# State copies, score steps and the last stores of a fused retention and GELU kernel: a change of places

What was changed: the copies of the states of the later chunk pair were put in the second half of a block, some pairs of score products were issued one step later, and in the last tile the rows of batches 2 and 3 (its half u = 0, "even half") were stored whole instead of in two halves of columns.

## The chip, the cores and the metric

One core of one Trainium2 chip. The metric is the time of one execution in microseconds of device time; lower is better. A profile gives a span some 1.7 us shorter than the timed run it belongs to. Runs that took over 1.5% longer than the fastest of their kernel would count as slow; all runs told of here are in the fast state, except one single run of unknown state that is marked where it is told.

## The reference

Eight batches of eight-head attention with a causal decay in place of a softmax, then a two-layer MLP with the tanh form of GELU on all 4608 rows:

```python
def _attn_ref(q, k, v):                    # q, k, v: (8, 8, 576, 64)
    scores = scale * np.matmul(q, k.transpose(0, 1, 3, 2))
    gamma = 1.0 - 2.0 ** (-5.0 - np.arange(H))
    Dmat = np.where(rel >= 0, gamma[:, None, None] ** rel[None, :, :], 0.0)
    return np.matmul(scores * Dmat[None], v)

def _moe_ref(x, w_in, w_out):              # x: (4608, 512), w_in: (512, 2048)
    h = x @ w_in
    g = 0.5 * h * (1.0 + np.tanh(c * (h + 0.044715 * h * h * h)))
    return g @ w_out
```

## The kernel before

The retention is done in chunks of 128 rows with a running state. Each batch has four whole chunks and a tail of 64 rows. The MLP works through nine blocks `t` of 512 rows: eight of whole chunks, and a last one (t = 8) that gathers the tails. A block of t = 2 to 7 has 30 steps: 16 "up" steps (four 128x512 matmuls, then a GELU on ACT), then 14 "product" steps for the second layer, which is computed as seven half-size products of sums (a Strassen scheme), each for two halves `u`. Between steps, the attention of batch t + 1 is woven in, at step numbers that a table fixes:

```python
    def states(t, u, b, c, tag):                  # states of chunks c and c + 1
        def go():
            us = bank(tag, "us")
            for n in range(2):
                state(b, c + n, us, n)            # 8 matmuls
            for n in range(2):
                scan(b, c + n)                    # DVE: running state "ws"
        at(t, u, go)
        def sp(n, hl):                            # ACT: state into tbd / tbt, a copy of 0.40 us
            at(t, u + 2 + 2 * n + hl, lambda: spread(b, c + n, A.copy, (hl,)))
        ...
    def values(t, u, *xs):
        at(t, u, lambda: ([av(*x) for x in xs], [inter(*x[:2]) for x in xs]))
        for n, x in enumerate(xs):                # ACT: values into xT, which frees a PSUM bank
            at(t, u + 1 + n, lambda x=x: put(*x[:2]))
    ...
    for t in range(1, 7):
        b, e = t + 1, t - 3
        if t == 1:
            ...
            u0, u1, u2, u3 = 11, 17, 19, 25
            states(t, u0, b, 0, "B")
            scores(t, u0, (b, 0, ("t0", "t1")), (b, 1, ("t2", "A")))
        else:
            u0, u1, u2, u3 = (8, 14, 19, 25) if t == 2 else (7, 13, 19, 25) if t == 3 else (6, 12, 19, 25)
            ...
            scores(t, u0, (b, 0, ("t0", "t1")), (b, 1, ("t2", "A" if t > 2 else "C")), *tail)
        states(t, u1, b, 2, "t0")
        values(t, u1, (b, 0, "t1"), (b, 1, "t2"), ...)
        scores(t, u2, (b, 2, ("hp", "hp")), (b, 3, ("t1", "t2")))
        if t < 6:
            states(t, u3, b + 1, 0, "t0")
        values(t, u3, (b, 2, "t1"), (b, 3, "t2"))
```

The products of the second half need activation sums that DVE makes from the GELU outputs; product 6 is the first that needs the second sum:

```python
    nc.vector.tensor_tensor(out=s["1"], in0=a21, in1=a22, op=ALU.add)            # L488
    nc.vector.tensor_tensor(out=s["2"], in0=s["1"], in1=a11, op=ALU.subtract)    # L489
```

The stores of the last tile, one 64-row half per queue:

```python
        def end(o, i, v, d=slice(0, DM)):
            b = 4 * v + 2 * i
            for h, e in enumerate((nc.sync, nc.scalar)):
                r0 = S * (b + h) + M0
                e.dma_start(out=out[r0 : r0 + TL, d], in_=o[TL * h : TL * h + TL, d])
        ...
        elif m == 7:
            ...
            if last:
                add(keep["o1"][:, u, HD:DM], keep["u3"][:, u], keep["o1"][:, u, HD:DM])
                end(keep["o1"][:, u], 1, u, slice(HD, DM))
        ...
        elif m == 4:
            if last:
                add(keep["o1"][:, u, 0:HD], keep["s1"][:, u], pr("B")[:, u])
                end(keep["o1"][:, u], 1, u, slice(0, HD))
```

Lines that come up in the profile: L317 score matmuls, L338 states, L359 state copies, L367 and L388 values, L405 value copies, L415 up matmuls, L421 their GELU, L488 and L489 the activation sums, L508 products, L523 adds of products, L536 stores of the last tile.

Of the kernel before, what the change touches and what calls it, by code (L numbers as in the profile page):

```python
# [19 lines left out]
def kernel(  # L20
# [12 lines left out]
    NT, DM = out.shape  # L33
# [30 lines left out]
    def bank(tag, name, dt=F32):  # L64
        if tag == "att":
            tag = "t" + str(turns["n"] % 3)
            turns["n"] += 1
        return ps.tile([128, 512 if dt == F32 else 1024], dt, tag=tag, name=name, bufs=BUFS[tag])
# [130 lines left out]
    for h in range(H):  # L199
        u = 64 * (h % 2)  # L200
# [132 lines left out]
    def state(b, c, us=None, n=0):  # L333
        a = att[b]
        us = bank("att", "us") if us is None else us
        for p in range(HP):
            for hl in range(2):
                nc.tensor.matmul(  # L338
                    us[64 * hl : 64 * hl + 64, 256 * n + 64 * p : 256 * n + 64 * p + 64],
                    a["k"][:, col(c, p, hl)],  # L340
                    a["v"][:, col(c, p, hl)],
                    start=True, stop=True,
                )
        a["U", c] = us[:, 256 * n : 256 * n + 256]

    def scan(b, c):
        a = att[b]
        uc = a.pop(("U", c)).rearrange("p (q d) -> p q d", d=64)
        if c > 0:
            s = sb.tile([128, HP, 64], F32, tag="vs", name="vs", bufs=2)  # L350
            nc.vector.tensor_tensor(out=s, in0=uc, in1=a["w"], op=ALU.add)
            uc = s
        a["w"] = a["w", c] = w = sb.tile([128, HP, 64], F32, tag="ws", name="ws", bufs=2)
        nc.vector.tensor_tensor(out=w, in0=uc, in1=gt, op=ALU.mult)  # L354

    def spread(b, c, cp, hls=(0, 1)):
        for hl in hls:
            r = slice(64 * hl, 64 * hl + 64)
            cp(out=(tbd[b % 2][r, c, :, r] if c < NC - 1 else tbt[b % 4][r, :, r]), in_=att[b]["w", c][r])  # L359
# [85 lines left out]
    def ost():  # L445
        return sb.tile([128, 2, DM], F32, tag="ost", name="ost", bufs=2)
# [17 lines left out]
    HD = DM // 2  # L464
# [48 lines left out]
    keep = {}  # L513

    def after(t, m, u):
        last = t == NTB - 1
        if u == 0 and not (last and m in (6, 7, 4)):
            return
        us = slice(u, u + 1) if last and m in (6, 7, 4) else slice(0, 2)
        def pr(tag):  # L520
            return op[tag, u].rearrange("p (u d) -> p u d", u=2)
        def add(o, a, b):
            nc.vector.tensor_tensor(out=o, in0=a, in1=b, op=ALU.add)  # L523
        def send(o, i):
            if t < B:
                nc.sync.dma_start(
                    out=out[S * t : S * t + TB, :].rearrange("(u i p) d -> p u i d", u=2, i=2)[:, :, i, :], in_=o
                )
                return
            for v in range(2):  # L530
                end(o[:, v], i, v)
# [5 lines that stand above are left out]
        if m == 1:  # L537
            keep["s1"] = sb.tile([128, 2, HD], F32, tag="k1", name="k1", bufs=1)
            nc.scalar.copy(out=keep["s1"], in_=pr("A"))
        elif m == 6:  # L540
            if us.start == 0:
                keep["u2"] = sb.tile([128, 2, HD], F32, tag="k2", name="k2", bufs=1)
            add(keep["u2"][:, us], keep["s1"][:, us], pr("B")[:, us])
        elif m == 7:
            if us.start == 0:
                keep["u3"] = sb.tile([128, 2, HD], F32, tag="k3", name="k3", bufs=1)
            add(keep["u3"][:, us], keep["s1"][:, us], pr("B")[:, us])
            if last:
                add(keep["o1"][:, u, HD:DM], keep["u3"][:, u], keep["o1"][:, u, HD:DM])
                end(keep["o1"][:, u], 1, u, slice(HD, DM))  # L550
                return
            keep["o1"] = ost()
            add(keep["o1"][:, :, HD:DM], keep["u3"], pr("C"))
        elif m == 5 and last:
            keep["o1"] = ost()
            nc.scalar.copy(out=keep["o1"][:, :, HD:DM], in_=pr("C"))
        elif m == 2:
            keep["o0"] = ost()
            nc.scalar.copy(out=keep["o0"][:, :, 0:HD], in_=pr("A"))  # L559
        elif m == 3:  # L560
            add(keep["o0"][:, :, HD:DM], keep["u2"], pr("C"))
            send(keep["o0"], 0)
        elif m == 4:
            if last:
                add(keep["o1"][:, u, 0:HD], keep["s1"][:, u], pr("B")[:, u])
                end(keep["o1"][:, u], 1, u, slice(0, HD))
            else:
                add(keep["o1"][:, :, 0:HD], keep["s1"], pr("B"))
                send(keep["o1"], 1)
# [25 lines left out]
    V, P, A = nc.vector, nc.gpsimd, nc.scalar  # L595
# [48 lines left out]
    def at(t, u, f):  # L644
        if t > 0 and u > 29:
            t, u = t + 1, u - 30
        events.setdefault((t, u), []).append(f)
# [31 lines left out]
    def scores(t, u, *xs):  # L679
        at(t, u, lambda: [score(*x) for x in xs])  # L680

    def states(t, u, b, c, tag):
        def go():
            us = bank(tag, "us")
            for n in range(2):
                state(b, c + n, us, n)
            for n in range(2):
                scan(b, c + n)
        at(t, u, go)
        def sp(n, hl):  # L690
            at(t, u + 2 + 2 * n + hl, lambda: spread(b, c + n, A.copy, (hl,)))
        for n in range(2):
            for hl in range(2):
                sp(n, hl)

    def values(t, u, *xs):
        at(t, u, lambda: ([av(*x) for x in xs], [inter(*x[:2]) for x in xs]))
        for n, x in enumerate(xs):
            at(t, u + 1 + n, lambda x=x: put(*x[:2]))
# [7 lines left out]
    def turns_of(t, u, b, c, tag):  # L707
        at(t, u, lambda: turn(b, c, A.copy, tag))
# [9 lines left out]
    for t in range(1, 7):  # L718
        b, e = t + 1, t - 3
        if t == 1:  # L720
            for c, (u, tag) in enumerate(((7, "t2"), (9, "A"), (15, "C"), (17, "hp"))):
                turns_of(t, u, b, c, tag)
            u0, u1, u2, u3 = 11, 17, 19, 25
            states(t, u0, b, 0, "B")
            scores(t, u0, (b, 0, ("t0", "t1")), (b, 1, ("t2", "A")))
        else:
            u0, u1, u2, u3 = (8, 14, 19, 25) if t == 2 else (7, 13, 19, 25) if t == 3 else (6, 12, 19, 25)
            tail = [(e, NC, ("B", "C"))] if e >= 0 else []
            scores(t, u0, (b, 0, ("t0", "t1")), (b, 1, ("t2", "A" if t > 2 else "C")), *tail)
        states(t, u1, b, 2, "t0")  # L730
        values(t, u1, (b, 0, "t1"), (b, 1, "t2"), *([(e, NC, "C")] if e >= 0 else []))
        scores(t, u2, (b, 2, ("hp", "hp")), (b, 3, ("t1", "t2")))
        if t < 6:
            states(t, u3, b + 1, 0, "t0")
        values(t, u3, (b, 2, "t1"), (b, 3, "t2"))
# [5 lines left out]
    for b in range(2, B):  # L741
        ent = chunks(b)
        eng = {"k": P, "q": P, "v": A}
        if b == 2:
            t0, ut = 1, [1, 1, 2, 4, 4, 5, 9, 9, 10, 13, 13, 14]
        else:
            t0, ut = b - 2, [16, 16, 17, 18, 18, 19, 20, 20, 22, 22] + ([27, 28] if b == NPE else [22, 23])
# [77 lines left out]
```

## Time and profile before

| | before |
|---|---|
| time, median of 3 runs | 304.36 us (304.33 to 305.08) |
| span of the profile | 302.8 us |
| tensor engine busy | 291.9 us |

To follow the argument, a reader needs one measure more, the length of a block: from the start of the first up matmul of block t to that of block t + 1, in the timeline of the tensor engine. In the profile before, blocks 2 to 7 last 30.11, 30.45, 30.79, 31.37, 30.84 and 28.77 us.

One place the prediction tells without its rows: the last activation sums of t = 6, on DVE, and what GpSimd (POOL) does beside them. Columns are start, duration, engine, line and operation:

```profile
229.38 1.22 POOL L83 DMA_DIRECT2D lt<-in_v_dram  x2 [1.99 <-ACT ev L244]
230.40 0.44 DVE L488 TENSOR_TENSOR s<-gT 128x512 f16<-128x512 f16 x1 [2.28 <-ACT gT L421]
230.61 0.69 POOL L257 TENSOR_TENSOR ek<-lt,sc 128x256 f16<-128x256 f32 x1
230.87 0.72 DVE L489 TENSOR_TENSOR s<-s,gT 128x512 f16<-128x512 f16 x1
```

GpSimd first issues loads (DMA_DIRECT2D), then casts. The sum that product 6 waits for starts while a GpSimd cast runs and takes 0.72 us.

### The profile page before, as it was taken

How to read it: one execution, taken by the hardware profiler on the slowest of the kernel's cores; microseconds unless marked ns; L12 is line 12 of the kernel's file. 1: busy time of each engine (PE TensorE's matmuls, PEld its weight loads, DVE VectorE, ACT ScalarE, POOL GpSimd, SP SyncE). 2: the span in 40 equal slices, each digit the busy share in tenths (PEclk: the TensorE clock that was granted, in tenths of full speed). 3: DMA queues.
4: the chain of work that ended last, by engine and by line, in shares of the span. 5: the costliest groups of instructions: out<-in, count | busy, mean ns of one | idle time of the engine just before them, and what ended most of it. 6: DMA issues, size and time to landing. Idle time of an engine off the chain costs nothing.

```text
span 302.8 us, 6867 instructions
## 1 busy us (share of the span) xinstructions
PE 291.9 (96%) x2747; PEld 197.4 (65%) x2747; DVE 175.9 (58%) x359; ACT 173.0 (57%) x332; POOL 120.2 (40%) x178
## 2 busy tenths in 40 slices
PE   6899999999999999999999999999999999999994
PEld 2568755788784588458845884578456844784583
DVE  6650879678962866386547653855396435342423
ACT  6676417998657573658366736593647246316620
POOL 8668315550924179106910591049757110000000
PEclk9999999999999999999999999999999999999998
DMA  7999999999999996999599959953962140103004
GB/s 203 216 296 391 387 286 224 203 263 242 201 189 230 201 261 125 221 208 255 100 219 209 239 66 203 225 133 65 276 79 60 32 157 11 26 20 121 2 0 139
DMA packets 130592, 52.87 MB, mean 175 GB/s; under 512 B 118785, under 2 KB 121345, under 8 KB 130561
## 3 DMA queue, kind: packets, MB, share of 16 engines
q1 hardware_dynamic: 128544, 48.77, 74.2%
q0 software_dynamic: 1536, 3.15, 4.6%
q10 hardware_dynamic: 480, 0.52, 0.6%
q8 instruction: 21, 0.34, 0.5%
q14 instruction: 11, 0.08, 0.1%
HBM read 36.70 MB, written 9.44 MB: 152 GB/s over the span
## 4 chain that ended last, share of the span: by engine, by line
PE 74%; ACT 9%; DMA 5%; SPq 4%; POOL 3%; issue 2%; DVE 1%; POOLq 0%
PE hp L415 28%; PE opB L508 11%; PE opC L508 8%; PE hp L432 7%; PE opA L508 6%; PE op L451 4%; SPq L95 3%; DMA tt<-cq 3%; PE st L317 3%; PE xs L367 2%; ACT gT L421 2%; DMA ld<-in_moe_w_in_dram 2%; PE xs L388 2%; ACT xT L405 1%; PE us L338 1%
## 5 line engine op out<-in xcount | busy, mean ns | idle before, releaser
L415 PE MATMUL hp<-xT,w_in_sb 128*128 128x512 f16 x448 | 101.2, 379 | 0.3
L421 ACT ACTIVATE gT<-hp 128x512 f16<-128x512 f32 x112 | 66.9, 598 | 54.8 <-PE hp L415 46.6
L415 PEld LDWEIGHTS <-w_in_sb 128*128 128x128 f16 x448 | 42.9, 98 | 50.9 <-issue 3.2
L508 PEld LDWEIGHTS <-gT 128*128 128x128 f16 x512 | 49.9, 98 | 7.4
L324 DVE TENSOR_TENSOR ret<-st,cm 128x512 f16<-128x512 f32 x64 | 40.0, 683 | 8.4 <-PE st L317 8.4
L488 DVE TENSOR_TENSOR s<-gT 128x512 f16<-128x512 f16 x32 | 14.7, 458 | 50.0 <-ACT gT L421 49.0
L257 POOL TENSOR_TENSOR ck<-ld,sc 128x512 f16<-128x512 f32 x31 | 32.9, 1062 | 21.3 <-DMA ld<-in_k_dram 18.7
L508 PEld LDWEIGHTS <-s 128*128 128x128 f16 x384 | 36.5, 98 | 6.2 <-DVE s L489 1.6
L508 PE MATMUL opA<-w_out_sb,gT 128*128 128x256 f16 x256 | 30.6, 273 | 0.0
L508 PE MATMUL opB<-wt,gT 128*128 128x256 f16 x256 | 30.4, 273 | 0.0
L432 PE MATMUL hp<-xT,w_in_sb 128*128 128x256 f16 x256 | 29.8, 273 | 0.4 <-POOL w_in_sb L582 0.2
L432 PEld LDWEIGHTS <-w_in_sb 128*128 128x128 f16 x256 | 24.6, 98 | 3.7 <-POOL w_in_sb L582 0.5
L257 POOL TENSOR_TENSOR cq<-ld,sc 128x512 f16<-128x512 f32 x24 | 25.2, 1052 | 2.6 <-DMA ld<-in_q_dram 2.5
L751 POOL COPY gate<-s 128x1 f16<-128x1 f16 x5 | 0.9, 187 | 62.3 <-DVE s L491 62.3
L559 ACT COPY ost<-opA 128x512 f32<-128x512 f32 x8 | 4.7, 587 | 31.8 <-PE opA L508 31.8
L438 ACT ACTIVATE gT<-hp 128x512 f16<-128x512 f32 x32 | 19.0, 600 | 5.9 <-PE hp L432 5.8
L405 ACT CAST xT<-xs 128x512 f16<-128x512 f32 x32 | 18.5, 582 | 4.1 <-PE xs L388 3.8
L359 ACT CAST tbd<-ws 64x256 f16<-64x256 f32 x48 | 19.3, 402 | 1.3 <-DVE ws L354 0.5
L523 DVE TENSOR_TENSOR ost<-k,opC 128x512 f32<-128x512 f32 x15 | 10.3, 687 | 16.4 <-PE opC L508 16.1
L523 DVE TENSOR_TENSOR k<-k,opB 128x512 f32<-128x512 f32 (+1 forms) x18 | 11.3, 629 | 12.4 <-PE opB L508 10.5
L508 PE MATMUL opB<-wt,s 128*128 128x256 f16 x128 | 15.8, 273 | 0.8 <-DVE s L489 0.8
L244 ACT CAST cv<-ld 128x512 f16<-128x512 f32 x27 | 15.8, 616 | 0.3
(96 smaller groups left out, 368.1 us busy)
## 6 DMA issues: line engine op xcount, KB each, us to landing
ld<-in_q_dram SPq DMA_DIRECT2D x32, 256.0 KB, 5.2
ld<-in_k_dram SPq DMA_DIRECT2D x32, 256.0 KB, 5.2
ld<-in_v_dram SPq DMA_DIRECT2D x32, 256.0 KB, 5.1
out_dram<-ost SPq DMA_DIRECT2D x16, 512.0 KB, 5.2
ld<-in_moe_w_in_dram SPq DMA_DIRECT2D x16, 256.0 KB, 5.9
ld<-in_moe_w_out_dram SPq DMA_DIRECT2D x16, 256.0 KB, 5.4
lt<-in_k_dram POOLq DMA_DIRECT2D x16, 64.0 KB, 4.7
lt<-in_q_dram POOLq DMA_DIRECT2D x16, 64.0 KB, 4.5
```

The costliest lines, as they stand in the source:

```text
L244: eng.copy(out=dst, in_=raw)
L257: eng.tensor_tensor(out=dst.rearrange("p (h d) -> p h d", d=D), in0=raw.rearrange("p (h d) -> p h d", d=D), in1=sc[:, s0 : s0 + nh].unsque ...
L324: nc.vector.tensor_tensor(out=r, in0=st[hl][:, 0:w], in1=m.rearrange("p n i -> p (n i)"), op=ALU.mult)
L359: cp(out=(tbd[b % 2][r, c, :, r] if c < NC - 1 else tbt[b % 4][r, :, r]), in_=att[b]["w", c][r])
L405: nc.scalar.copy(out=xT[:, g0 : g0 + 2], in_=src)
L415: nc.tensor.matmul(hp.rearrange("p (g t) -> p g t", t=TL), w_in_sb[:, ct, 128 * fc : 128 * fc + 128], xT[:, o : o + TB // TL, ct, :], star ...
L421: nc.scalar.activation(out=gT[t][:, fc].rearrange("p i n -> p (i n)"), in_=hp, func=AF.Gelu_apprx_tanh)
L432: nc.tensor.matmul(hp[:, 256 * x : 256 * x + 256].rearrange("p (g t) -> p g t", t=TL), w_in_sb[:, ct, 128 * (f + x) : 128 * (f + x) + 128] ...
L438: nc.scalar.activation(out=gT[t][:, f : f + 2, 2 * u : 2 * u + 2, :].rearrange("p f i n -> p f (i n)"), in_=hp.rearrange("p (f n) -> p f n ...
L488: nc.vector.tensor_tensor(out=s["1"], in0=a21, in1=a22, op=ALU.add)
L508: nc.tensor.matmul(op[tag, u][:, HD * u : HD * u + HD], lhs(f), rhs[:, f], start=(new and (u == 0 or own) and f == 0), stop=(f == NH - 1), ...
L523: nc.vector.tensor_tensor(out=o, in0=a, in1=b, op=ALU.add)
```

## The change

The intent: the late state copies should leave ACT free for the last GELU of a block and for the copies that free a bank; a pair of scores one step later should find its inputs ready; and fewer store issues at the end should get the last one out earlier.

```diff
@@ after(): stores of the last tile
-                end(keep["o1"][:, u], 1, u, slice(HD, DM))
+                if u:
+                    end(keep["o1"][:, u], 1, u, slice(HD, DM))
...
-                end(keep["o1"][:, u], 1, u, slice(0, HD))
+                end(keep["o1"][:, u], 1, u, slice(0, HD if u else DM))
@@ states
-    def states(t, u, b, c, tag):
+    def states(t, u, b, c, tag, wait=2):
-            at(t, u + 2 + 2 * n + hl, lambda: spread(b, c + n, A.copy, (hl,)))
+            at(t, u + wait + 2 * n + hl, lambda: spread(b, c + n, A.copy, (hl,)))
@@ schedule of t = 1 to 6
-            u0, u1, u2, u3 = 11, 17, 19, 25
+            u0, u1, u2, u3 = 11, 17, 20, 25
-            u0, u1, u2, u3 = (8, 14, 19, 25) if t == 2 else (7, 13, 19, 25) if t == 3 else (6, 12, 19, 25)
+            u0, u1, u2, u3 = (8, 14, 19, 25) if t == 2 else (7, 13, 19, 25)
-        states(t, u1, b, 2, "t0")
+        states(t, u1, b, 2, "t0", 6)
```

## The prediction

> **What bounds the kernel now.** I read the page first (busy shares, slices, chain), then the waits of the tensor engine, then its timeline around each wait and at the end of the span. From the page:
>
> ```profile
> span 302.8 us, 6867 instructions
> PE 291.9 (96%) x2747; PEld 197.4 (65%) x2747; DVE 175.9 (58%) x359; ACT 173.0 (57%) x332; POOL 120.2 (40%) x178
> ...
> PE 74%; ACT 9%; DMA 5%; SPq 4%; POOL 3%; issue 2%; DVE 1%; POOLq 0%
> ```
>
> The tensor engine is busy 96% of the span at full granted clock and carries 74% of the chain that ended last; no other engine reaches 60%. A change that removes no matmul can win only the engine's pauses and what lies after its last matmul. The view of waits on the tensor engine names the pauses:
>
> ```profile
> PE opB L508 <- DVE s L489: 0.8, 3, 0.5
> ...
> PE st L317 <- DMA tt<-cq: 0.5, 1, 0.5
> PE st L317 <- ACT xT L405: 0.5, 1, 0.5
> ```
>
> These five are what this change can touch; the waits for L217, L287, L273 and L432 in the same view belong to the opening. Their true size is read from starts, because the view takes the end of a matmul from a model: a 256-column matmul is given 273 ns, yet sixteen of them advance by 1.75 us in the chain, 0.109 each. The tensor engine's timeline, for the blocks that start at 150, 181 and 212 us (t = 4, 5, 6) and for block t = 1:
>
> ```profile
> 150.26 6.43 PE L415 MATMUL hp<-xT,w_in_sb 128*128 128x512 f16 x28
> 156.62 0.62 PE L317 MATMUL st<-tt 64*128 64x128 f16 x16
> ...
> 168.19 0.82 PE L508 MATMUL opB<-wt,s 128*128 128x256 f16 x6
> 169.18 1.27 PE L508 MATMUL opB<-wt,s 128*128 128x256 f16 x10 [0.17 <-DVE s L489]
> ```
> ```profile
> 181.05 6.43 PE L415 MATMUL hp<-xT,w_in_sb 128*128 128x512 f16 x28
> 187.99 0.62 PE L317 MATMUL st<-tt 64*128 64x128 f16 x16 [0.51 <-DMA tt<-cq]
> ...
> 199.57 0.82 PE L508 MATMUL opB<-wt,s 128*128 128x256 f16 x6
> 200.55 1.27 PE L508 MATMUL opB<-wt,s 128*128 128x256 f16 x10 [0.17 <-DVE s L489]
> ```
> ```profile
> 78.32 0.45 PE L317 MATMUL st<-tt 64*128 64x128 f16 x9
> 79.27 0.38 PE L317 MATMUL st<-tt 64*128 64x128 f16 x7 [0.50 <-ACT xT L405]
> 79.58 1.92 PE L508 MATMUL opC<-wt,s 128*128 128x256 f16 x16
> ```
>
> Six matmuls of 0.109 advance 0.655 us. In t = 4 the seventh starts 0.99 after the first: 0.33 lost. In t = 5 it is 0.98: 0.33 lost. In t = 6 the same pair of rows starts at 230.35 and 231.64: 1.29, so 0.64 lost. The scores of t = 5 start 6.94 after their block, those of t = 4 6.36 after theirs: 0.58 lost for the transposed q. The sixteen score matmuls of t = 1 take 1.26 to the next product, those of t = 4 take 0.55 (170.38 to 170.93): 0.71 lost. Sum 2.59 us.
>
> **What the Trainium skill says.** "Perfetto Trace Analysis", section "Tensor Engine Instruction (MATMUL, LD_WEIGHTS)", says that the end of a matmul is estimated and that ACT, DVE and GpSimd work strictly in order. The trace agrees with both: 273 ns shown against a step of 109, and the last GELU of a block standing behind copies that nobody needs yet. "DMA: Bandwidth & Descriptors", section "Anatomy of one DMA — SWDGE (gpsimd) path", puts the fixed part of a transfer at about 2.0 us, mostly the write receipt, and says that a wait on a semaphore happens on the issuing sequencer; the final stores of this trace land 1.9 to 3.4 us after issue. "SBUF — State Buffer", section "Who interferes with whom", says that a DVE operation with two SBUF inputs can block against a GpSimd operation that reads SBUF: in t = 6 the second activation sum took 0.72 us beside a GpSimd cast, against 0.42 in t = 4.
>
> **The change part by part.** No matmul, copy or byte is added or removed; only two DMA issues go. Every effect is one of place.
>
> (a) Blocks t = 4 to 6 do their first scores after step 7 instead of 6, and the states and values after 13 instead of 12. Block t = 3 already runs at 7 and 13, with the same tail work, and its timeline has none of the waits: starts of the blocks from that timeline are 119.81, 150.26, 181.05 and 212.42, so t = 3 lasts 30.45, t = 4 30.79 and t = 5 31.37. The differences, 0.34 and 0.92, are the losses found above. In t = 3 the last GELU (ACT timeline) starts at 136.75, 16.94 after its block; in t = 4 at 167.61, 17.35 after. This 0.41 covers 0.33. For t = 6 it covers 0.41 of 0.64; part (b) helps with the rest.
>
> For the scores of t = 5, one step later is four matmuls of 0.2165, 0.87, against a wait of 0.58. The transposes start from a gate at the end of the activation sums of t = 4, and this moves too: 0.71 by the gain in t = 1 and 0.41 by the earlier GELU. By the landing records they land at 187.91; then at about 186.8. The tensor engine arrives at 187.41 - 0.71 - 0.33 + 0.87 = 187.2. Slack 0.4, so the wait goes.
>
> (b) The copies of the chunk 2 and 3 states go from 2 to 5 steps after the states to 6 to 9. Four copies of 0.40 leave the place between the last GELU and the copies of the values. In t = 4 one stood ahead of the last GELU (166.83). They land where ACT idles 3.1 to 4.0 us before it copies out product 2, and 1.6 us fits. Alone this would also cure the 0.33 of t = 4 and 5; it overlaps with (a) and is not counted twice. It leaves t = 6 about 0.1 lost, because the sum there still meets the GpSimd cast.
>
> (c) Block t = 1 does its second scores at step 20 instead of 19. One step there is eight matmuls of 0.109, 0.87, more than 0.71; and (b) takes a state copy from between the two value copies it waits for. All 0.71 goes. The order of instructions shows that a weight sum now runs on DVE ahead of the four masks: 1.43 before. Masks then end near 83.0, and the values that need them start at 84.4 after the gain.
>
> (d) At the end each queue makes five store issues instead of six. The trace before:
>
> ```profile
> 294.61 3.66 PE L508 MATMUL opB<-wt,gT 128*128 128x256 f16 x32
> ...
> 295.62 3.77 SPq L536 DMA_DIRECT2D out_dram<-ost  x6
> 295.63 4.56 ACTq L536 DMA_DIRECT2D out_dram<-ost  x6
> ...
> 298.30 0.42 DVE L523 TENSOR_TENSOR ost<-k,opB 128x256 f32<-128x256 f32 x1 [0.45 <-PE opB L508]
> ```
>
> The last add ends at 298.78 in unrounded starts, SP issues the last store at 298.89, ACT only at 299.77: the event before it waits for a semaphore of ACT's second store, which landed at 299.69. Semaphores are reused in a ring of eight for twelve issues. With ten, the last pair reuses those of the first pair, landed at 298.10 and 298.42, before the add is done. So ACT's last issue should come at about 298.9, 0.9 earlier. Not all of that shows: the 1.05 MB of stores land from 297.8 on, and the landings follow each other by 0.2 to 0.5 us per pair, so the transfer engines are near full. SP's last store landed at 301.08, ACT's at 301.70; with the same bytes the new last one lands near 301.3, and SP clears two or three more semaphores after it at 0.06 each. I count 0.3, not 0.9.
>
> Sum: 2.59 less 0.2 for remnants (t = 6, and a margin on t = 5) is 2.4; with 0.3 from the end, 2.7. 304.36 - 2.7 = 301.7 us, 0.9%.
>
> **The rivals.** First, the transposes of t = 5 keep their landing time (held by transfers ahead of them rather than by the gate). Then the tensor engine, arriving at 187.2, waits as before, and a later block adds nothing: 302.3. For it: those transposes are 9.3 us from issue to landing, the longest of the five. Against it: the chain of waits goes gate, eight GpSimd casts, transposes, without a pause for anything else.
>
> Second, the late copies become a wait. Chunk 2's state is needed by the values at step 25, now four steps after its copy; if ACT stood behind a cast that waits for a load, the values would stop. Against it: ACT shows no wait for loads in these blocks and idles over 3 us before step 25. In t = 1 the chunk 3 copies now come after the copy of product 2 and push the copies of the values by some 0.25; the next block's inputs still come early. If it happened in every block, 0.4 each would return 2 us: 303.7.
>
> Third, the end: the whole rows of the last tile's even half leave one product later, so 131 KB are moved from an earlier to a later, fuller time. If the transfer engines lose that time, 0.4 us, the end gains nothing: 302.0. If they are not full, it gains 0.8: 301.2.
>
> **Range and chances.** With everything the time is about 301.0; with rivals one and three together and some copies in the way, about 302.8. So 301.7, from 300.9 to 302.8, 8 times in 10. Faster by 2% needs 6.1 us; the pauses that remain outside the opening are the bubbles of 0.09 when the matmul kind changes, which stay. Chance 0.02. Slower by 2% needs a new wait of 6 us, which nothing shows: 0.01. Within 2%: 0.97.
>
> **What would show it.** The view of waits should have lost all five waits of the second fence, or keep under 0.2 for L489 in t = 6. Blocks t = 4 and 5 should last 30.4 to 30.5 like t = 3, t = 6 about 30.2 to 30.3. ACT's last store should be issued within 0.2 of SP's and wait for no landing. The first rival would show as a wait of L317 for the transposed q near 184 to 187; the second as a wait of L388 or L367 for ACT near step 25; the third as last landings that keep 2.9 us from the last add. I am wrong if the span falls by under 1.5 us, or if a new row in the view of waits is over 0.3.

## The result and the profile after

302.47 us, median of 4 runs (302.17 to 303.03), against 304.35 us for the kernel before (304.20 to 305.08, 4 runs): 1.88 us less. Ratio 0.9936, 95% interval 0.9914 to 0.9957. A ratio here is the mean time of one kernel's fast runs over that of the other's of the same rounds, so it is not quite the ratio of the medians. In microseconds the interval is a gain of 1.3 to 2.6: clear of the noise, but far from 2%.

The page of the changed kernel, and its view of waits on the tensor engine (us in total, times, longest):

```profile
span 301.3 us, 6865 instructions
PE 290.9 (97%) x2747; PEld 196.9 (65%) x2747; DVE 174.6 (58%) x359; ACT 172.7 (57%) x332; POOL 120.2 (40%) x178
...
PE 86%; SPq 4%; ACT 3%; DMA 2%; issue 2%; DVE 1%; POOL 0%
```
```profile
PE opB L508 <- DVE s L489: 0.4, 1, 0.4
PE fill L217 <- ACT xT L405: 0.2, 1, 0.2
PE hp L415 <- ACT gT L421: 0.2, 1, 0.2
```

The chain that ended last is now 86% tensor engine (before 74%), because it no longer leaves for ACT and the transposes. Of the five waits in the prediction's second fence, four are gone and one is left. The row of L415 is new in the view, but its pause is not: it lies in block 7, at 244.04, and was 0.15 us before, 0.165 now. The timeline of the tensor engine in t = 1, then in t = 5, then in t = 6:

```profile
80.01 0.62 PE L317 MATMUL st<-tt 64*128 64x128 f16 x16
80.57 1.05 PE L508 MATMUL opC<-wt,s 128*128 128x256 f16 x8
```
```profile
180.81 7.29 PE L415 MATMUL hp<-xT,w_in_sb 128*128 128x512 f16 x32
188.04 0.62 PE L317 MATMUL st<-tt 64*128 64x128 f16 x16
...
198.75 1.91 PE L508 MATMUL opB<-wt,s 128*128 128x256 f16 x16
```
```profile
229.19 0.82 PE L508 MATMUL opB<-wt,s 128*128 128x256 f16 x6
230.37 1.27 PE L508 MATMUL opB<-wt,s 128*128 128x256 f16 x10 [0.36 <-DVE s L489]
```

In t = 1 the sixteen score matmuls take 0.56 us to the next product, where it was 1.26. In t = 5 the scores follow 7.23 after their block, the 32 up matmuls ahead of them and nothing more, and product 6 runs through without a break. In t = 6 it still breaks after six matmuls: 1.18 from row to row, where 0.655 would be clean, so 0.52 is lost (before 0.64). The DVE and GpSimd rows of t = 6 say beside what:

```profile
228.10 1.22 POOL L83 DMA_DIRECT2D lt<-in_v_dram  x2 [2.28 <-ACT ev L244]
228.82 0.73 DVE L488 TENSOR_TENSOR s<-gT 128x512 f16<-128x512 f16 x1 [1.61 <-ACT gT L421]
229.33 0.69 POOL L257 TENSOR_TENSOR ek<-lt,sc 128x256 f16<-128x256 f32 x1
229.59 0.72 DVE L489 TENSOR_TENSOR s<-s,gT 128x512 f16<-128x512 f16 x1
```

Before, only the second of the two sums was long. Now both are. The GELU came 0.42 earlier in its block, the GpSimd work only 0.12, so they meet more fully.

The end of the span, to be set against the fourth part of the prediction:

```profile
294.36 3.60 SPq L536 DMA_DIRECT2D out_dram<-ost  x5
294.37 3.89 ACTq L536 DMA_DIRECT2D out_dram<-ost  x5
...
297.04 0.42 DVE L523 TENSOR_TENSOR ost<-k,opB 128x256 f32<-128x256 f32 x1 [0.45 <-PE opB L508]
```

ACT's issues end 0.3 after SP's, where it was 0.8. In unrounded records ACT's last store is issued 0.22 after the end of the last add (before 0.99), but its landing comes 2.65 after that add (before 2.93).

Where the time went, from the two profiles:

| stretch | before | after | gain |
|---|---|---|---|
| start to the first product of t = 1 (nothing changed here) | 73.13 | 73.96 | -0.83 |
| from there to block 2 | 16.57 | 15.86 | 0.71 |
| block 2 | 30.11 | 30.11 | 0 |
| block 3 | 30.45 | 30.45 | 0 |
| block 4 | 30.79 | 30.45 | 0.34 |
| block 5 | 31.37 | 30.45 | 0.92 |
| block 6 | 30.84 | 30.73 | 0.11 |
| block 7 and the last tile, to the last matmul | 54.74 | 54.75 | -0.01 |
| last matmul to the start of the last instruction | 4.71 | 4.53 | 0.18 |
| that instruction | 0.05 | 0.05 | 0 |
| span | 302.75 | 301.31 | 1.44 |

The parts that the change touches gave 2.26 us in this pair. The 0.83 lost in the opening has nothing to do with it: over the fourteen profiles the first product of t = 1 starts anywhere from 73.13 to 74.55 us, while the clean blocks come out alike to 0.02. In this pair all of the difference arises before 22 us, where the tensor engine waits for the first inputs and weights to be cast on GpSimd: in the view of waits L287 for k went from 0.8 to 1.2, L432 for the weights from 0.2 to 0.7, L273 for q from 0.4 to 0.7. So the experiments below are judged by their block lengths first and by the timed ratio second.

### The profile page after: what moved, and what is told of

The parts are those of the page before. It is cut to its first block, busy times and chain, and to the rows that moved or that the text cites. A ratio compares the mean times of both kernels' runs of the same rounds, so it can differ in the third digit from the quotient of the medians.

```text
span 301.3 us, 6865 instructions
## 1 busy us (share of the span) xinstructions
PE 290.9 (97%) x2747; PEld 196.9 (65%) x2747; DVE 174.6 (58%) x359; ACT 172.7 (57%) x332; POOL 120.2 (40%) x178
## 4 chain that ended last, share of the span: by engine, by line
PE 86%; SPq 4%; ACT 3%; DMA 2%; issue 2%; DVE 1%; POOL 0%
PE hp L415 32%; PE opB L508 13%; PE opC L508 9%; PE opA L508 9%; PE hp L432 8%; PE op L451 4%; SPq L95 3%; PE st L317 3%; PE xs L367 3%; PE xs L388 2%; DMA ld<-in_moe_w_in_dram 2%; PE us L338 2%; PE tr L287 1%; ACT gT L438 1%; SPq L89 1%
## 5 line engine op out<-in xcount | busy, mean ns | idle before, releaser
L415 PE MATMUL hp<-xT,w_in_sb 128*128 128x512 f16 x448 | 101.2, 379 | 0.3 <-ACT gT L421 0.2
L415 PEld LDWEIGHTS <-w_in_sb 128*128 128x128 f16 x448 | 42.9, 98 | 50.9 <-issue 3.2
L432 PE MATMUL hp<-xT,w_in_sb 128*128 128x256 f16 x256 | 29.9, 273 | 0.8 <-POOL w_in_sb L583 0.7
L432 PEld LDWEIGHTS <-w_in_sb 128*128 128x128 f16 x256 | 24.6, 98 | 4.3 <-POOL w_in_sb L583 1.1
L583 DVE CAST w_out_sb<-ld 128x512 f16<-128x512 f32 x16 | 8.9, 579 | 12.1 <-DMA ld<-in_moe_w_out_dram 12.0
```

Source lines behind the costliest of these rows:

```text
L415: nc.tensor.matmul(hp.rearrange("p (g t) -> p g t", t=TL), w_in_sb[:, ct, 128 * fc : 128 * fc + 128], xT[:, o : o + TB // TL, ct, :], star ...
L432: nc.tensor.matmul(hp[:, 256 * x : 256 * x + 256].rearrange("p (g t) -> p g t", t=TL), w_in_sb[:, ct, 128 * (f + x) : 128 * (f + x) + 128] ...
```

## The experiments

All blocks in one table, in us; "t = 1" is from its first product to block 2, "end" from the start of the last matmul to the start of the last instruction of the span, 0.05 before the span ends ("the end of the span"). Block 7 is 28.77 to 28.79 and the last tile 25.96 in every one.

| kernel | t = 1 | 2 | 3 | 4 | 5 | 6 | end | ratio to before (95%) |
|---|---|---|---|---|---|---|---|---|
| before | 16.57 | 30.11 | 30.45 | 30.79 | 31.37 | 30.84 | 4.71 | |
| changed | 15.86 | 30.11 | 30.45 | 30.45 | 30.45 | 30.73 | 4.53 | 0.9936 (0.9914 to 0.9957) |
| only_u01 | 16.57 | 30.11 | 30.45 | 30.45 | 30.45 | 30.72 | 4.66 | 0.9949 (0.9923 to 0.9976) |
| only_u2 | 15.86 | 30.11 | 30.45 | 30.79 | 30.78 | 30.84 | 4.63 | 0.9973 (0.9941 to 1.0005) |
| only_wait | 16.27 | 30.11 | 30.45 | 30.49 | 30.57 | 30.84 | 4.66 | 0.9960 (0.9936 to 0.9984) |
| only_tail | 16.57 | 30.11 | 30.45 | 30.78 | 31.19 | 30.84 | 4.48 | 0.9980 (0.9953 to 1.0006) |
| after_again | 15.86 | 30.11 | 30.45 | 30.45 | 30.45 | 30.73 | 4.56 | 0.9949 (0.9934 to 0.9963) |
| after_wait2 | 15.86 | 30.11 | 30.45 | 30.45 | 30.48 | 30.73 | 4.47 | 0.9952 (0.9932 to 0.9973) |
| after_gate6 | 15.86 | 30.11 | 30.45 | 30.45 | 30.45 | 30.19 | 4.44 | 0.9930 (0.9913 to 0.9947) |
| after_gate6_o0 | 15.86 | 30.11 | 31.47 | 30.45 | 30.45 | 30.19 | 4.88 | 0.9940 (0.9923 to 0.9957) |
| tail_pool | 16.56 | 30.11 | 30.45 | 30.79 | 30.78 | 30.84 | 5.29 | 1.0033 (1.0013 to 1.0054) |
| gate6_w1 | 15.86 | 29.92 | 30.26 | 30.26 | 30.26 | 30.01 | 4.39 | 0.9897 (0.9882 to 0.9912) |
| gate6_w1_u8 | 15.86 | 29.92 | 30.26 | 30.26 | 30.26 | 30.01 | 4.57 | 0.9889 (0.9873 to 0.9906) |

### Each part alone

The steps of blocks 4 to 6 alone (only_u01):

```diff
-            u0, u1, u2, u3 = (8, 14, 19, 25) if t == 2 else (7, 13, 19, 25) if t == 3 else (6, 12, 19, 25)
+            u0, u1, u2, u3 = (8, 14, 19, 25) if t == 2 else (7, 13, 19, 25)
```

> The kernel before with one edit: blocks t = 4 to 6 take the steps of t = 3 (first scores after 7, states and values after 13). Main theory: this edit alone gives the whole gain of blocks 4 and 5, which then last 30.45 us as in the changed kernel (before: 30.79 and 31.37), so the state copies need not move for it. Rival: the state copies that stand ahead of the last GELU were the cause, and blocks 4 and 5 keep 0.2 to 0.3 us each for the second activation sum. For t = 6 (before 30.84, changed 30.73) the main theory says 30.6 to 30.9 since the sum still meets the GpSimd cast. Time 1.2 to 1.5 us under before, +-0.5 for the opening.

Measured: blocks 4 and 5 at 30.45, block 6 at 30.72, the rest as before; median 303.48 against 304.56. The theory holds to 0.01, the rival falls. In its view of waits the stall of t = 1 and that of t = 6 are left:

```profile
PE st L317 <- ACT xT L405: 0.5, 1, 0.5
PE hp L432 <- POOL w_in_sb L582: 0.4, 1, 0.4
PE opB L508 <- DVE s L489: 0.4, 1, 0.4
```

The second scores of t = 1 alone (only_u2):

```diff
-            u0, u1, u2, u3 = 11, 17, 19, 25
+            u0, u1, u2, u3 = 11, 17, 20, 25
```

> The kernel before with one edit: second scores of block t = 1 one step later. Main theory: the stall of 0.66 us at the scores of t = 1 goes completely and nothing else changes: from the first product of t = 1 to the start of block 2 it is 0.7 us less than before. Rival: without the later state copies the value copy that the scores wait for stays late and 0.2 us or more of the stall remains. Blocks 2 to 7 as before within 0.05 us. Time 0.7 us under before, +-0.5.

Measured: 16.57 to 15.86, all 0.71, without help from the state copies. One thing the expectation did not have: block 5 lasts 30.78 instead of 31.37, though nothing in it or in block 4 was edited. Its scores did not wait for the transposed q at all in this profile; the scatter of that wait is told below.

The late state copies alone (only_wait):

```diff
-    def states(t, u, b, c, tag):
+    def states(t, u, b, c, tag, wait=2):
-            at(t, u + 2 + 2 * n + hl, ...)
+            at(t, u + wait + 2 * n + hl, ...)
-        states(t, u1, b, 2, "t0")
+        states(t, u1, b, 2, "t0", 6)
```

> The kernel before with one edit: the copies of the later states 6 steps after the states instead of 2. Main theory: one copy of 0.40 us leaves the place ahead of the last GELU, so the waits for the second activation sum in t = 4 and t = 5 (0.33 each) go; the wait for the transposed q in t = 5 stays at 0.4 to 0.6 because the gate and the tensor engine both move; block 4 lasts 30.45, block 5 30.9 to 31.1; the stall of t = 1 falls by 0.3 to 0.4. Rival: the copies do not matter, blocks 4 and 5 keep 30.79 and 31.37. Time 1.0 us under before, +-0.5.

Measured: the waits for the second sum in t = 4 and 5 go, t = 1 gains 0.30. Block 5 came out at 30.57, under the 30.9 to 31.1 expected: the wait for the transposed q was about 0.1 and not 0.4 to 0.6. In t = 6 nothing was gained at all.

The stores alone (only_tail):

```diff
-                end(keep["o1"][:, u], 1, u, slice(HD, DM))
+                if u:
+                    end(keep["o1"][:, u], 1, u, slice(HD, DM))
-                end(keep["o1"][:, u], 1, u, slice(0, HD))
+                end(keep["o1"][:, u], 1, u, slice(0, HD if u else DM))
```

> The kernel before with one edit: the even half of the last tile stored as whole rows. From the start of the last matmul to the end of the span it was 4.71 us before and 4.53 in the changed kernel. Main theory: this edit alone makes that difference, 0.15 to 0.35 us; all blocks as before. Rival: the 0.18 was chance and the span after the last matmul is within 0.05 of before. Time 0.2 us under before, within the noise of 0.5.

Measured: 4.48, 0.23 less than before. All profiles together settle that it is no chance: with the old stores 4.71, 4.66, 4.63 and 4.66, with the new ones 4.39 to 4.57 in seven profiles, their means apart by some 0.17. Block 5, which no edit touches, came out at 31.19 instead of 31.37. In the timed runs it is within the noise.

### The wait for the transposed q is a scatter, not a constant

The three misses on block 5 point the same way. From the landing records: when the last byte of the transposed q for the scores of t = 5 lands, counted from the start of block 4. In the old steps the tensor engine is ready for the scores 37.1 to 37.2 after that start (a block of 30.79 and 6.36 more; 36.9 in only_wait, whose block 4 is 30.49).

| before | only_u2 | only_wait | only_tail | tail_pool | after | only_u01 | after_again | after_wait2 | after_gate6 |
|---|---|---|---|---|---|---|---|---|---|
| 37.60 | 36.65 | 36.80 | 37.41 | 36.63 | 36.15 | 37.18 | 36.14 | 37.57 | 36.85 |

The issue follows the gate by the same time in all of them: 7.2 us for the transposes of k, 8.6 for those of q. What scatters is the time from issue to landing, from 8.3 to 9.7 us over all fourteen profiles. In the old steps the wait was 0.58, 0, 0.1, 0.4 and 0. In the new ones the scores come near 37.7, and only after_wait2 came close (0.03 lost). So the later step removes a wait that was there in three profiles of five and averaged some 0.2 us, and the 0.58 in the profile before was the largest of the five. What the landing scatters with was not looked for.

### The state copies back in their old place

```diff
-        states(t, u1, b, 2, "t0", 6)
+        states(t, u1, b, 2, "t0")
```
on the changed kernel, with that kernel run again beside it.

> The changed kernel once more, as the partner of the other three. Theory: blocks 2 to 6 last 30.11, 30.45, 30.45, 30.45 and 30.73 us again to 0.02, the part after the last matmul 4.5; all that differs from run to run lies before 35 us. Time 1.6 to 2.2 us under before.

> The changed kernel with the state copies put back to 2 steps after the states. Main theory: the other edits cover the same waits, so blocks 1 to 6 last what they last in the changed kernel to 0.05 us and the time is the same to 0.1%. Rival: the move was needed, and block 1 (scores of the second pair) or block 6 gets 0.1 to 0.4 us longer.

Measured: every block alike but block 5 (30.48 against 30.45, the scatter just told); 302.80 against 302.88. The move of the state copies, which the change's name puts first, adds nothing once the steps are moved. Alone it would have gained what only_wait shows. The changed kernel itself came out 1.6 us under before in this set (302.88 against 304.47), a little less than in the first.

### What holds block 6

The last activation sums of t = 6 run beside GpSimd, which issues loads for the next tail and casts the tail. To part them, a one-column GpSimd copy that reads the last sum is put ahead of that work, and the tail's loads are put after it:

```diff
+    at(6, 16, lambda: nc.gpsimd.tensor_copy(out=gate, in_=gs[6]["4"][:, NH - 1, 1, 0:1]))
-    TAILS |= {5: ((6, 15), (6, 24), (6, 24)), ...
+    TAILS |= {5: ((6, 17), (6, 24), (6, 24)), ...
```

> The changed kernel with GpSimd held in block t = 6: a one-column copy that reads the last activation sum goes ahead of the loads of the next tail, so the two GpSimd casts of that tail cannot run beside the last activation sums. Main theory: the 0.52 us left in t = 6 comes from DVE sums stretched from 0.43 to 0.73 each by GpSimd casts; they return to 0.43, the wait goes, block 6 lasts 30.2 and the kernel gains 0.5 us over the changed one. Rival: the sums are stretched by something else (descriptor writing for loads, ACT), or the wait is for the GELU itself: block 6 stays at 30.5 to 30.75. Block 7 must stay at 28.8, or the later tail has become a wait.

Measured: block 6 at 30.19, 0.53 less than in the changed kernel; block 7 unchanged at 28.77; 302.35 against 302.88. The rows that answer to those of the changed kernel, DVE and tensor engine:

```profile
228.26 0.43 DVE L488 TENSOR_TENSOR s<-gT 128x512 f16<-128x512 f16 x1 [2.11 <-ACT gT L421]
228.62 1.91 PE L508 MATMUL opB<-wt,s 128*128 128x256 f16 x16
228.72 0.42 DVE L489 TENSOR_TENSOR s<-s,gT 128x512 f16<-128x512 f16 x1
```

The sums are back at 0.43 and 0.42, and product 6 runs through in one row of sixteen. That GpSimd's work in this place, with the loads that it issues, stretches them is shown. Which part of it does, the casts or the issuing of loads, is not: the gate moves both. By the spans recorded neither alone fits. In the changed kernel the first sum, at 0.43, would have been done at 229.25, before the cast starts at 229.33, and yet it took 0.73; in the profile before, a sum at 225.30 lay wholly beside the issuing of loads (224.93 to 226.17) and took 0.42. But the spans on GpSimd are rough.

### What holds the end

Two experiments asked whether the bytes or the last store itself hold the end, and one went further in the direction of the change. Together they leave it open.

Fewer issues still, on the kernel with the gate: the first pair of the last tile in one issue of 256 KB per queue:

```diff
-            for v in range(2):
-                end(o[:, v], i, v)
+            for h, e in enumerate((nc.sync, nc.scalar)):
+                e.dma_start(
+                    out=out.rearrange("(v w s) d -> w s v d", v=2, s=S)[2 * i + h, M0:S],
+                    in_=o[TL * h : TL * h + TL],
+                )
```

> The same, and the first pair of the last tile stored by one issue per queue instead of two (256 KB each), so that each queue makes four store issues at the end and no semaphore is used twice. Main theory: the end is held by bytes still moving, which now start up to 0.6 us earlier; from the last matmul to the end 4.2 to 4.4 instead of 4.53. Rival: the last store's own fixed time holds it, and it stays within 0.05 of 4.5. Time 0.6 to 0.8 us under the changed kernel.

Measured: a miss. The end took 4.88, longer than with ten issues; the last landing came 2.87 after the last add instead of 2.56 (medians 302.54 and 302.35, 6 runs each). It is one profile. Its landings show that the bytes left later and not earlier: the first pair's last landing came 1.08 after the last add, against 0.75 with two issues per queue. The same profile shows the scatter of transposes at its worst, in block 3, which no edit touches:

```profile
PE st L317 <- DMA tt<-cq: 1.0, 1, 1.0
```

Their landing came 38.22 after the start of block 2, where the other profiles have 36.1 to 36.9; the scores come at 37.3.

The early half-rows through a third queue, on the kernel before, so that ACT and SP make five issues each and the bytes still leave early:

```diff
-        def end(o, i, v, d=slice(0, DM)):
+        def end(o, i, v, d=slice(0, DM), es=(nc.sync, nc.scalar)):
-            for h, e in enumerate((nc.sync, nc.scalar)):
+            for h, e in enumerate(es):
-                end(keep["o1"][:, u], 1, u, slice(HD, DM))
+                end(keep["o1"][:, u], 1, u, slice(HD, DM), (nc.sync, nc.scalar) if u else (nc.gpsimd, nc.gpsimd))
```

> The kernel before with one edit: the early half-row stores of the last tile's even half go through the GpSimd queue, so SP and ACT make five issues each as in the changed kernel, but these 131 KB still leave at their early time. It parts the two sides of the end. Theory: the late issue on ACT was the semaphore ring and goes (ACT's last issue within 0.3 us of SP's); the bytes then decide, and as they leave early the last landing comes 2.2 to 2.5 us after the last add (before 2.92, changed 2.65), 4.2 to 4.4 us from the last matmul to the end. Rival: the end is the fixed time of the last store, and it comes out at 4.5 as in the changed kernel.

Measured: half of it. ACT's last issue comes 0.21 after the last add and 0.19 after SP's: the late issue of before was the ring of semaphores. But the last landing comes 2.78 after the add, no earlier than in the changed kernel, and the program then ends 1.83 after that landing instead of 1.20: a DRAIN on GpSimd lasts until 1.05 after it. The kernel is slower than before by a third of a percent (2 runs).

Fewer bytes, on the changed kernel, with a wrong result (three quarters of the first pair's columns are not stored):

```diff
-                end(o[:, v], i, v)
+                end(o[:, v, 0:128], i, v, slice(0, 128))
```

> Wrong result on purpose: the changed kernel, with only 128 of the 512 columns of the last tile's first pair stored. The ten issues and their places stay, 393 KB of the last 1.05 MB go. If moving bytes hold the end, the last landing comes 0.4 us or more earlier than the 2.5 to 2.7 us after the last add of eight profiles with ten issues (at 2.2 or below). If the fixed time of the last store holds it, it stays at 2.5 to 2.7.

Measured (one run, state unknown, 302.53 us; result wrong as meant): the last landing comes 2.57 after the last add, among the 2.52 to 2.67 of the seven other profiles with ten issues. By the expectation that would be the fixed time of the last store. But the bytes that were cut are not those that could hold the end. The view of stretches, 1 us before the last add's end and 2 us after it, in the changed kernel and then here; the last two numbers are the busy share of the 16 DMA engines and GB/s:

```profile
296.46:297.46 1.00, 0.55 (x5) 0.24 (x3) 0.55 (x2) 0.00 (x0) 0.00 (x0) 1.00 0.85 299
297.46:299.46 2.00, 0.00 (x0) 0.00 (x0) 0.00 (x1) 0.00 (x0) 0.00 (x0) 0.89 0.88 262
```
```profile
296.01:297.01 1.00, 0.54 (x5) 0.23 (x3) 0.55 (x2) 0.00 (x0) 0.00 (x0) 1.00 0.10 27
297.01:299.01 2.00, 0.00 (x0) 0.00 (x0) 0.00 (x0) 0.00 (x0) 0.00 (x0) 0.92 0.87 241
```

The cut emptied the time before the last add (0.85 to 0.10). After it the engines are as full as before (0.88 and 0.87): by the packets in the traces that start after it, 498 KB were still to move, against 528. In this run all of them are the second pair's, as the first pair's last landing came 2.26 before the add. So the run shows only that the first pair's bytes do not hold the end. That bytes left after the last add matter is suggested by after_gate6_o0: 678 KB were left there, the share in the 2 us after it was 0.94 and the last landing came at 2.87. No run cut the second pair's bytes, so it is not shown. tail_pool does not settle it either: 526 KB were left after its last add.

Between issue and landing ACT's last store took 1.94 when it went out 0.87 after SP's (before), 2.43 when it went out 0.19 after SP's (changed) and 2.35 here. The 0.77 that the earlier issue won is lost for the most part in a slower landing, beside engines that are still at work on the other stores.

### Further than the change

Every block from 2 to 6 still has a pause of 0.185 us near its start, where the fourth up step waits for a bank. ACT in the changed kernel at the start of block 2:

```profile
90.94 0.60 ACT L421 ACTIVATE gT<-hp 128x512 f16<-128x512 f32 x1 [0.95 <-PE hp L415]
91.56 0.40 ACT L359 CAST tbd<-ws 64x256 f16<-64x256 f32 x1
91.98 1.26 ACT L421 ACTIVATE gT<-hp 128x512 f16<-128x512 f32 x2
```

A state copy stands between the first two GELUs. It is the last of the four copies of the first chunk pair; one step earlier it is ahead of the block:

```diff
-            states(t, u3, b + 1, 0, "t0")
+            states(t, u3, b + 1, 0, "t0", 1)
```

> The version with GpSimd held in t = 6, and the copies of the first states of the next block 1 step after the states instead of 2, so that none stands between the first two GELUs of a block. Theory: the pause of 0.185 us near the start of blocks 2 to 6 is the product waiting for a bank whose GELU stands behind that copy; it goes, and these blocks last 29.92, 30.26, 30.26, 30.26 and 30.0. Time 0.9 us under the version with GpSimd held, 3.0 us under before. Rival: the copy, now ahead of the value copies, delays those and a pause comes back at the block start.

Measured: blocks 2 to 6 at 29.92, 30.26, 30.26, 30.26 and 30.01, as expected to 0.01; 301.60 against 304.86. The same rows of ACT now:

```profile
91.10 0.60 ACT L421 ACTIVATE gT<-hp 128x512 f16<-128x512 f32 x1 [0.54 <-PE hp L415]
91.90 0.60 ACT L421 ACTIVATE gT<-hp 128x512 f16<-128x512 f32 x1 [0.21 <-PE hp L415]
```

The last one gives the scores one more step:

```diff
-            u0, u1, u2, u3 = (8, 14, 19, 25) if t == 2 else (7, 13, 19, 25)
+            u0, u1, u2, u3 = (8, 14, 19, 25)
```

> The same with blocks t = 3 to 6 on the steps of t = 2 (first scores after 8, states and values after 14). Theory: the landings of the transposes scatter over 1.8 us from run to run in the same code, and in one profile in ten they cost t = 3 a full 1.02 us; another step of 0.87 covers all but the rarest, so blocks stay at their clean length and the runs scatter less. Block lengths as the version without it. Rival: the value copies come behind the last GELU and a bank is then late: a new wait of 0.2 to 0.6 per block at the second activation sum or at the second scores.

Measured: the same blocks to 0.01, no new wait; 301.17 us, ratio 0.9889 to before, the fastest kernel. It was 0.43 under the version without the edit, but the profiles put that into the opening (73.17 against 74.12) and not into a block, so the gain of this edit is not shown; that it makes no block longer is. That the runs scatter less does not show either: the four lie 0.66 apart, those without the edit 0.44.

## Why the prediction was right or wrong

The time was 302.5 where 301.7 was predicted, inside the range; the gain 1.9 where it was 2.7. The steps (a) and (c) were right in their mechanism; two terms were too large, and the width of the range, 1.9 us, took them in.

- **Step (a), the steps of blocks 4 and 5: right.** The model that they would become like block 3 holds to 0.01 us, and only_u01 shows that this edit alone does it.
- **The 0.58 for the transposed q: the size was that of one profile.** The gate moved as said (0.41 earlier in its block) and the wait went. But the prediction took the landing for a fixed time after the gate. It scatters by 1.4 us, and the average wait in the old steps was some 0.2. If these five profiles are typical, the term is worth about a third of what was counted (an estimate: 0.2 of 0.58). This is also what became of the first rival: it named transfers ahead of the transposes as the danger, and the landing does vary, only the later step covers nearly all of it.
- **Step (b), the state copies: right that they overlap with (a), wrong on t = 6.** "It leaves t = 6 about 0.1 lost" is the step that failed: 0.52 was lost. The prediction added an earlier GELU to one stretched sum. In the run the earlier GELU put both sums into GpSimd's work, and each took 0.3 longer. after_gate6 shows it by taking that work away: 0.53 back.
- **Step (c), t = 1: right**, 0.71 predicted and 0.71 measured. The copies were not needed for it.
- **Step (d), the end: right on the issue; its reason for the small gain fits the trace.** ACT's issue came earlier by 0.77 (0.9 predicted), and 0.18 came out at the end (0.3 predicted). The reason given, transfer engines near full, agrees with their share of 0.88 in the 2 us after the last add; no edit has shown that it is the cause. The clearing of two more semaphores after the last landing, 0.06 each, is in the profile as said. The prediction's "unrounded" times and its landings are counted from a zero 0.05 us earlier than the views; its differences within them stand.
- **What it left out.** It said that outside the opening only bubbles of 0.09 would remain. There was also a pause of 0.185 near the start of each of blocks 2 to 6, which gate6_w1 took away.
- **The rivals.** The second, late copies that become a wait, did not happen in any block. The third, 131 KB moved to a fuller time, stays open: the gain of 0.18 lies between the 0 that it gave and the 0.8 without it, and no run took these bytes out of the time after the last add.
- **Its own signs.** Blocks 4 and 5 at 30.45 and ACT's last store 0.19 after SP's came as said. Against it came L489 in t = 6, with 0.4 in the view of waits where 0.2 was allowed, and the span, which fell by 1.44 where under 1.5 was to mean wrong; without the 0.83 of the opening it would have been 2.26.

By the trace: 0.71 + 0.34 + 0.92 + 0.11 + 0.18 = 2.26 where 2.7 was predicted; the missing 0.44 is t = 6 for the most part. The measured 1.9 is 0.4 less again. The usual size of the wait for the transposed q would account for it (0.58 less 0.2), but this is not shown: the interval of 1.3 to 2.6 holds both, and the opening, which is in both kernels, scatters by more.

## What to carry to other kernels

In a kernel that is bound by one engine, measure the length of each repeated stretch on that engine from starts, and compare a stretch that has a wait with one that is laid out alike and has none: the clean one told here what the edit gave to a hundredth in blocks 4 and 5, and missed by half a microsecond in block 6, where something else ran beside it. A wait for a transfer that is seen once is one draw; look at its landing in several profiles before it is counted in full. And when an instruction is moved earlier to end a wait, ask what else on the shared parts of the core it will then run beside.

## What the Trainium skill lacked or had wrong

- "TensorE: Matmul & The Clock Gate", section "Back-to-back issue gap", gives about 131 ns per matmul of 512 columns as measured in sustained streams, and calls 216 ns an over-count. Here the up matmuls, each with its weight load, advance 0.2165 us at full granted clock (32 in 7.23 us with their pauses), and 256-column products 0.109. The isolated figures of the same section fit, the sustained one doesn't.
- "DMA: Bandwidth & Descriptors", section "Anatomy of one DMA — SWDGE (gpsimd) path", gives one fixed part of about 2.0 us, for GpSimd's path. It has no figure for how much later a store lands while others are moving. Here ACT's last store of 64 KB took 1.94 us to land in the four profiles in which it went out last by some 0.8 us, and 2.28 to 2.46 in the eight with ten issues, in which it went out 0.2 after SP's.
- The same page does not say how much a DMA transpose's time to landing varies. Here the transpose of q for t = 5 landed 8.3 to 9.7 us after issue in fourteen profiles, the one for t = 3 after 7.3 to 8.2 and once after 9.4, which made a wait of 1.0 us.
- No page that I read has the cost of running out of completion semaphores: with twelve stores on eight of them, the last issue stood 0.87 us behind the other queue's for a landing it had no use for.
- "SBUF — State Buffer", section "Who interferes with whom", says that a DVE operation with two SBUF inputs contends with a GpSimd operation that reads SBUF. The runs agree (0.72 against 0.42 us, and 0.42 again with GpSimd held). One sum was stretched to 0.73 while GpSimd was for the most part issuing loads, by its rough spans, and another beside such issuing took 0.42; whether that contends too, these runs leave open.
